# First pair of chunks by eight plain products, weights narrowed on VectorE alone, and the sums of squares queued behind the score products

## The chip, the cores and the metric

The kernel runs on one core of a Trainium2 chip. Its time is the device time of one execution in microseconds (us). The five engines work side by side, each through its own queue in order: TensorE (PE in the profile, with PEld for its weight loads), VectorE (DVE), ScalarE (ACT), GpSimd (POOL) and SyncE (SP), whose queue issues all the transfers here. A matrix product goes to a PSUM bank, and DVE or ACT take it from there.

## The reference

Four batches of a channel attention feed one Gelu layer pair. `q`, `k`, `v` have the shape (4, 6080, 256); everything is fp32, and the weights arrive as fp64.

```python
qn = q / (np.linalg.norm(q, axis=1, keepdims=True) + 1e-06)
kn = k / (np.linalg.norm(k, axis=1, keepdims=True) + 1e-06)
s = kn.transpose(0, 2, 1) @ qn / tau          # 256 x 256 per batch
a = softmax(s)                                # rows, with 1e-09 in the denominator
x = (v @ a).reshape(24320, 256)
h = x @ w_in                                  # 256 -> 2048
g = 0.5 * h * (1.0 + erf(h / sqrt(2)))
return g @ w_out                              # 2048 -> 256
```

The kernel multiplies `a` into `w_in` first (W = a @ w_in, 256 x 2048 per batch), so each batch is two large products around a Gelu, h = v @ W and out = g @ w_out.

## The kernel before

**Precision.** A product of two fp32 matrices is made of fp32r matmuls on a high and a low part of each operand: high by high, high by low and low by high, three matmuls for one product (`product`, L443, and L518 to L520). A split is a cast on ACT (`hi`) and a subtraction on DVE (`lo`). The products of the first batch's scores are plain fp32 (L147).

**The score stage (batch 0).** `qk_first(js)` runs for 24 steps `js`. A step takes a 512 KB block `raw` of `k` and `q` rows and adds four products to the two score blocks `s` in PSUM. For the first 16 steps (`NSQ`) `squares` squares the block on ACT and adds it on DVE to `acc`; the norms' remaining rows come from `norm_part`, which loads a piece `kq` of 1024 columns and sums its squares on ACT (L212). At step 18 (`NSQ + 2`) `sum_up` (L175) sums `acc` over the partitions by eight one-column products with a vector of ones, into `nps`. Blocks for 13 steps are loaded ahead; in the same queue of SP stand the `kq` pieces, the first `v` block, and the fp64 weight blocks ("units").

**The softmax** is a generator of stages; between them `qk_fill` gives PE the first four steps of the next batch's scores (16 products, L164). Stage one copies the scores from PSUM and adds the sums of squares, the next makes the reciprocal norms, then come the scaling with a product `rq` (L322), the exponential (L333), and transposes into `eh` and `el`.

**Weights.** `narrow(hi, lo, raw, eng)` makes an fp32r pair from one fp64 unit of 128 x 512 without fp64 arithmetic: clamp (L237), square on ACT (L239), shift and merge of the bits (L242, L244), a mask (L246), the exponent (L249), the tail (L251 on DVE, or L254 on ACT and L255 on POOL), a cast on ACT (L256), and two last steps on POOL (L257, L258). There are 16 units, eight of `w_in` (four groups of two) and eight of `w_out`; `NARROWS` says behind which score steps the first five are narrowed, and `paces` how many follow behind each unit of the first pair of chunks. Every third of these has its tail made on DVE (`VEC`). `keep` writes the pairs to DRAM for later chunks. Working tiles are `nt` at first, and `kqc` (two buffers) later.

`w_group(b, g)` multiplies `eh`, `el` with `win` for a quarter of the 2048 features (12 matmuls, L369 to L371), scales it out of PSUM into four blocks A11, A12, A21, A22 and forms the four sums S1 to S4. Seven of the eight, without A21, are split into `whs`, `wls`.

**Chunks.** The rows of a batch go in six pairs of chunks, each chunk up to 512 rows. `v_sums` forms T1 to T4 from the four blocks B of the pair's `v`, `v_split` splits the seven operands in `ORDER`. In `first_products` eight units `u` of 256 features each make the four blocks of h for two chunks by seven products instead of eight, a Strassen scheme in Winograd's form: three intermediate results are copied from PSUM by ACT (`p1`, `p5`, `u2`, L468) and added by DVE to later ones (`h`, L473). `gelu` makes `gh` and `g` on ACT (L456, L457) and `gl` on DVE (L458). Behind each product stands one group of three matmuls of the second layer for the unit before (`second_products`, L518 to L520).

**What sets the order.** The tile framework places each instruction in its engine's queue by program order and by its own estimate of readiness; single-buffered tiles and PSUM banks (four each for `ph` and `po`) add waits. `behind(name)` queues instructions behind a marked one, and `high_priority` puts the softmax and the first weight group forward. Transfers keep their order on SP, so a transfer that waits for a buffer holds those behind it.

Of the kernel before, what the change touches and what calls it, by code (L numbers as in the profile page):

```python
# [47 lines left out]

VEC = 3

TOP_MAX = (2.0 - 2.0 ** -3 - 2.0 ** -23) * 2.0 ** 16
TOP_MIN = 1.125 * 2.0 ** -15

A11, A22, A12, S1, S2, S3, S4 = range(7)
B11, B21, B22, T1, T2, T3, T4 = range(7)


@with_exitstack
def channel_attention_gelu_ffn(ctx, tc, qk, kqt, vt, tau, w_in, w_out, out):
# [80 lines left out]
    def qk_first(js):  # L140
        if js == 0:
            state["s"] = [bank()[:, 0:C] for m in range(NCT)]
        s = state["s"]
        raw = raws.pop((0, js))
        for j in range(JS):
            for m in range(NCT):
                nc.tensor.matmul(s[m], raw[:, j, 0, m * P:(m + 1) * P], raw[:, j, 1],  # L147
                                 start=(js == 0 and j == 0), stop=(js * JS + j == NJ - 1), skip_group_check=True)
# [74 lines left out]

    def narrow(hi, lo, raw, eng):

# [23 lines left out]
        nc.vector.tensor_scalar(out=body, in0=w.bitcast(U32), scalar1=0xFF800000, scalar2=None, op0=ALU.bitwise_and)  # L249
        if eng is nc.vector:  # L250
            eng.scalar_tensor_tensor(out=tail, in0=low, scalar=2.0 ** -52, in1=body.bitcast(F32), op0=ALU.mult,  # L251
                                     op1=ALU.mult)
        else:
            nc.scalar.activation(out=tail, in_=low, func=AF.Copy, scale=2.0 ** -52)  # L254
            eng.tensor_tensor(out=tail, in0=tail, in1=body.bitcast(F32), op=ALU.mult)  # L255
        nc.scalar.copy(out=hi, in_=w)  # L256
        nc.gpsimd.tensor_tensor(out=w, in0=w, in1=f32(hi), op=ALU.subtract)  # L257
        nc.gpsimd.tensor_tensor(out=lo, in0=w, in1=tail, op=ALU.add)  # L258

# [25 lines left out]
    def softmax(first, pool, name):  # L285
# [13 lines left out]
        nsum = state.pop("nsum")  # L299
        if first:  # L300
            nc.vector.reduce_sum(out=z, in_=nsum[:, :, NSQ // NSJ:NSC], axis=AX.X)
            nc.vector.tensor_tensor(out=x, in0=state.pop("nps")[:, 0:2 * NCT], in1=z, op=ALU.add)
        else:
            nc.vector.reduce_sum(out=x, in_=nsum[:, :, 0:NSC], axis=AX.X)
# [46 lines left out]


    def w_split(g, i, src):
        nc.scalar.copy(out=whs[g][:, i], in_=src)
        nc.vector.tensor_tensor(out=wls[g][:, i], in0=src, in1=f32(whs[g][:, i]), op=ALU.subtract)  # L355

    def w_group(b, g):
# [7 lines left out]
        for m in range(NCT):  # L365
            cs = slice(m * P, (m + 1) * P)
            pwt = bank()
            for d in range(NCT):
                nc.tensor.matmul(pwt, eh[:, d, cs], win[:, 0, d], start=(d == 0), stop=False)  # L369
                nc.tensor.matmul(pwt, eh[:, d, cs], win[:, 1, d], start=False, stop=False)  # L370
                nc.tensor.matmul(pwt, el[:, d, cs], win[:, 0, d], start=False, stop=(d == NCT - 1))  # L371
            nc.scalar.activation(out=tmp[:, 2 * m:2 * m + 2], in_=pwt.rearrange("p (q r c) -> p r q c", q=2, r=2),
                                 func=AF.Copy, scale=state["rden"][:, m:m + 1])
            if first and m == 0:
                w_split(g, A11, a11)
        tt = nc.vector.tensor_tensor
        if first:

            tt(out=s1, in0=a21, in1=a22, op=ALU.add)
            w_split(g, S1, s1)  # L380
            tt(out=s2, in0=s1, in1=a11, op=ALU.subtract)
            w_split(g, S2, s2)
            w_split(g, A12, a12)
            tt(out=s3, in0=a11, in1=a21, op=ALU.subtract)
            w_split(g, S3, s3)
            tt(out=s4, in0=a12, in1=s2, op=ALU.subtract)
            w_split(g, S4, s4)
            w_split(g, A22, a22)
# [38 lines left out]
    def v_split(b, p, i):  # L427
        n = PAIRS[p][1]
        x = v_blocks(b, p)
        src = {B11: x[0, 0], B21: x[1, 0], B22: x[1, 1]}.get(i)  # L430
        if src is None:
# [11 lines left out]
    def product(b, p, u, a, v, ps, start, stop):  # L443
        n = PAIRS[p][1]
        g, q = divmod(u, 2)
        hi, lo = vops[b, p, v]
        wh, wl = whs[g][:, a, q], wls[g][:, a, q]
        nc.tensor.matmul(ps[:, :n], wh, hi[:, :n], start=start, stop=False, skip_group_check=True)  # L448
# [3 lines left out]
    def gelu(src, n):  # L452
# [5 lines left out]
        nc.vector.tensor_tensor(out=gl[:, :n], in0=g[:, :n], in1=f32(gh[:, :n]), op=ALU.subtract)  # L458
        return gh, gl

    def first_products(b, p, u):
# [90 lines left out]

    def narrow_unit(eng):
        kind, g, d, raw = loaded.popleft()
        if kind == "in":
            if d == 0:
                new_win(0, g)
            win = wins[0, g]
            narrow(win[:, 0, d], win[:, 1, d], raw, eng)
            if d == NCT - 1:  # L560
                keep(keep_in[g], win)
        else:
            new_wo((0, 0, g))
            wo = wos[0, 0, g]
            narrow(wo[:, 0].rearrange("p f c -> p (f c)"), wo[:, 1].rearrange("p f c -> p (f c)"), raw, eng)
            keep(keep_out[g], wo)
# [5 lines left out]

    paces = (2, 1, 2, 2, 1, 1, 1)
    loaded = deque()
# [13 lines left out]
    for js in range(NQS):  # L588
# [7 lines left out]
        if js in NARROWS:  # L596
            narrow_unit(nc.gpsimd)
# [31 lines left out]
    load_unit()  # L629
    narrow_unit(nc.gpsimd)  # L630
    load_unit()
# [55 lines left out]
    for b, p, u in steps:  # L687
        pair = (b, p + 1) if p + 1 < NP else (b + 1, 0)
        for i, _ in enumerate(first_products(b, p, u)):
            next(second, None)  # L690
            if u == NU - 1 and pair[0] < B:
                v_split(*pair, ORDER[i][1])
# [4 lines left out]
        if (b, p) == (0, 0):  # L697
            for _ in range(paces[u] if u < len(paces) else 0):
                narrow_unit(nc.vector if len(units) % VEC == 0 else nc.gpsimd)
                if units:  # L700
# [33 lines left out]
```

## Time and profile before

| | |
|---|---|
| median of three runs | 2243.2 us (2242.62 to 2248.22) |
| the profiled execution | 2243.63 us, span 2241.8 us |
| granted TensorE clock, mean | 0.992 |
| busy: PE, DVE, ACT, POOL | 2190.7, 1410.7, 1451.9, 77.1 us |
| moved by transfers | 269.63 MB, mean 120 GB/s |

The span runs from the first instruction to the last; the rest of the execution's time lies around it. A busy PE need not be at its best rate: its records overlap, and at a lower granted clock they take longer. Where rows are shown, a timeline's columns are start, duration, engine, line, operation, tiles and shapes, with a count and, in brackets, the idle time before and what ended it; a group's are busy time and mean duration in nanoseconds, and then the idle time before. An x with a number is a count of instructions. An fp32 matmul leaves two records.

### The profile page before, as it was taken

The page shows a single profiled execution, that of the slowest core. Times are in us where ns is not written, and L with a number is a line of the kernel's source. Part 1 is how long each engine was busy: PE and PEld are TensorE (multiplying, and loading weights), DVE is VectorE, ACT ScalarE, POOL GpSimd, SP SyncE. Part 2 cuts the span into 40 slices and gives each one's busy share as a digit, 9 for nine tenths or more (in the row PEclk, how much of TensorE's full clock was granted, in tenths as well). Part 3 has the DMA queues.
Part 4 walks back from the last instruction along what each step waited for, and adds up shares of the span by engine and source line. Part 5 has one row for each costly group of instructions (what it writes and reads, how often), then busy time and mean ns, then how long its engine had stood idle before and what let it go on. Part 6 is the DMA issues. An engine that isn't in the chain of part 4 may idle for free.

```text
span 2241.8 us, 26294 instructions
## 1 busy us (share of the span) xinstructions
PE 2190.7 (98%) x9640; PEld 1795.2 (80%) x9640; DVE 1410.7 (63%) x2161; ACT 1451.9 (65%) x2637; POOL 77.1 (3%) x52
## 2 busy tenths in 40 slices
PE   7889999999999999999999999999999999999999
PEld 5667777888888888888888888888888888888888
DVE  6698466675666766756567666576566655555454
ACT  6467887565985656656666556566576666666665
POOL 3351000000000000000000000000000000000000
PEclk9899999999999999999999999999999999999999
DMA  9446766331573323323224232232122221221221
GB/s 349 176 149 217 229 231 211 109 116 62 187 237 111 123 85 104 122 82 105 76 94 138 87 123 103 85 121 81 62 86 84 90 88 48 94 85 51 90 68 53
DMA packets 77634, 269.63 MB, mean 120 GB/s; under 512 B 7744, under 2 KB 9792, under 8 KB 75456
## 3 DMA queue, kind: packets, MB, share of 16 engines
q1 hardware_dynamic: 77504, 267.94, 35.2%
q8 instruction: 76, 1.25, 0.2%
q14 instruction: 54, 0.44, 0.1%
HBM read 234.62 MB, written 33.29 MB: 120 GB/s over the span
## 4 chain that ended last, share of the span: by engine, by line
PE 80%; ACT 6%; DMA 4%; DVE 4%; issue 1%; POOL 0%; ACTq 0%; DVEq 0%; POOLq 0%
PE po L520 14%; PE po L518 13%; PE po L519 13%; PE ph L450 12%; PE ph L449 12%; PE ph L448 12%; DMA kqc<-kqt 4%; PE ph L194 2%; ACT kqc L212 2%; ACT gh L456 1%; ACT g L457 1%; PE ph L196 1%; DVE gl L458 1%; DVE h L473 1%; PE ph L370 0%
## 5 line engine op out<-in xcount | busy, mean ns | idle before, releaser
L458 DVE TENSOR_TENSOR gl<-g,gh 128x512 fp32r<-128x512 f32 (+1 forms) x768 | 529.0, 691 | 155.8 <-ACT g L457 152.9
L520 PE MATMUL po<-gh,wo 128*128 128x512 f32 (+1 forms) x1536 | 605.7, 394 | 0.0
L519 PE MATMUL po<-gl,wo 128*128 128x512 f32 (+1 forms) x1536 | 597.2, 389 | 3.3 <-DVE gl L458 3.3
L518 PE MATMUL po<-gh,wo 128*128 128x512 f32 (+1 forms) x1536 | 598.3, 390 | 0.0
L473 DVE TENSOR_TENSOR h<-ph,p 128x512 f32<-128x512 f32 (+1 forms) x384 | 262.5, 684 | 529.3 <-PE ph L450 415.4
L456 ACT ACTIVATE gh<-h 128x512 fp32r<-128x512 f32 (+1 forms) x576 | 360.7, 626 | 298.6 <-DVE h L473 295.8
L448 PE MATMUL ph<-vh,wh 128*128 128x512 f32 (+1 forms) x1344 | 528.3, 393 | 21.2 <-DVE h L473 8.9
L450 PE MATMUL ph<-vh,wl 128*128 128x512 f32 (+1 forms) x1344 | 527.3, 393 | 1.8 <-DVE wl L355 1.0
L449 PE MATMUL ph<-vl,wh 128*128 128x512 f32 (+1 forms) x1344 | 526.4, 392 | 0.0
L468 ACT COPY p<-ph 128x512 f32<-128x512 f32 (+1 forms) x384 | 222.4, 583 | 250.7 <-PE ph L450 250.4
L457 ACT ACTIVATE g<-h 128x512 f32<-128x512 f32 (+1 forms) x576 | 352.5, 612 | 0.0
L519 PEld LDWEIGHTS po<-gl,wo 128*128 128x128 f32 x1536 | 288.9, 188 | 69.6 <-DVE gl L458 5.6
L520 PEld LDWEIGHTS po<-gh,wo 128*128 128x128 f32 x1536 | 289.0, 188 | 61.4
L518 PEld LDWEIGHTS po<-gh,wo 128*128 128x128 f32 x1536 | 288.5, 188 | 61.8 <-ACT gh L456 0.6
L448 PEld LDWEIGHTS ph<-vh,wh 128*128 128x128 f32 x1344 | 253.5, 189 | 85.4 <-DVE h L473 13.3
L449 PEld LDWEIGHTS ph<-vl,wh 128*128 128x128 f32 x1344 | 253.8, 189 | 56.0
L450 PEld LDWEIGHTS ph<-vh,wl 128*128 128x128 f32 x1344 | 253.4, 189 | 54.4 <-DVE wl L355 1.4
L468 ACT COPY u<-ph 128x512 f32<-128x512 f32 (+1 forms) x192 | 111.6, 581 | 116.5 <-PE ph L450 116.5
L473 DVE TENSOR_TENSOR h<-ph,u 128x512 f32<-128x512 f32 (+1 forms) x192 | 131.1, 683 | 3.4
L457 ACT ACTIVATE g<-ph 128x512 f32<-128x512 f32 (+1 forms) x192 | 111.8, 582 | 0.0
L456 ACT ACTIVATE gh<-ph 128x512 fp32r<-128x512 f32 (+1 forms) x192 | 110.2, 574 | 0.0
L194 PE MATMUL ph<-hl 128*128 128x512 f32 x272 | 96.0, 392 | 0.0
(135 smaller groups left out, 1399.4 us busy)
## 6 DMA issues: line engine op xcount, KB each, us to landing
wo<-keep_out SPq DMA_DIRECT2D x184, 512.0 KB, 3.3
raw<-qk SPq DMA_DIRECT2D x95, 512.0 KB, 4.4
kqc<-kqt SPq DMA_DIRECT2D x72, 512.0 KB, 4.5
v_raw<-vt SPq DMA_DIRECT2D x20, 1024.0 KB, 5.0
out<-osb SPq DMA_DIRECT2D x40, 512.0 KB, 3.2
win<-keep_in SPq DMA_DIRECT2D x12, 1024.0 KB, 5.0
kq<-kqt SPq DMA_DIRECT2D x8, 512.0 KB, 7.6
raw<-w_out SPq DMA_DIRECT2D x8, 512.0 KB, 4.1
```

The costliest lines, as they stand in the source:

```text
L194: nc.tensor.matmul(s, hl[:, 0, j, 0, cs], hl[:, :, j, 1], start=(i == 0), stop=False, skip_group_check=True)
L448: nc.tensor.matmul(ps[:, :n], wh, hi[:, :n], start=start, stop=False, skip_group_check=True)
L449: nc.tensor.matmul(ps[:, :n], wh, lo[:, :n], start=False, stop=False, skip_group_check=True)
L450: nc.tensor.matmul(ps[:, :n], wl, hi[:, :n], start=False, stop=stop, skip_group_check=True)
L456: nc.scalar.activation(out=gh[:, :n], in_=src, func=AF.Gelu)
L457: nc.scalar.activation(out=g[:, :n], in_=src, func=AF.Gelu)
L458: nc.vector.tensor_tensor(out=gl[:, :n], in0=g[:, :n], in1=f32(gh[:, :n]), op=ALU.subtract)
L468: nc.scalar.copy(out=t[:, :n], in_=ps[:, :n])
L473: nc.vector.tensor_tensor(out=h[:, :n], in0=ps[:, :n], in1=t[:, :n], op=ALU.add)
L518: nc.tensor.matmul(o, wo[:, 0, i, cs], gh[:, :n], start=first, stop=False)
L519: nc.tensor.matmul(o, wo[:, 0, i, cs], gl[:, :n], start=False, stop=False)
L520: nc.tensor.matmul(o, wo[:, 1, i, cs], gh[:, :n], start=False, stop=last)
```

## The change

Three parts.

1. `sum_up` leaves step 18 of the scores. It is issued in the softmax's first stage, behind the mark `scores` that the last score product leaves.
2. `narrow` makes every tail on DVE (L251's form) and takes its two last steps from POOL to DVE. `paces` and the operands of `narrow_unit` follow.
3. The first pair of chunks of the first batch takes `plain_products`: eight products from A11, A12, A21, A22 and B11, B12, B21, B22, two to a block, with neither copies nor sums. So `v_sums` and three of the seven `v_split` fall away for this pair; `w_split` also makes A21 for the first batch's groups, in the tiles of T2 and T3 of the chunks (`w_slot`); and the first group's S sums are formed and split behind its four plain blocks. The later pairs are as before.

```diff
+A21, B12 = -1, T1
+PLAIN = (((1, 0), ((A11, B11), (A12, B21))), ((0, 0), ((A21, B11), (A22, B21))),
+         ((1, 1), ((A11, B12), (A12, B22))), ((0, 1), ((A21, B12), (A22, B22))))
...
-                nc.tensor.matmul(s[m], raw[:, j, 0, m * P:(m + 1) * P], raw[:, j, 1], ...
+                marks["scores"] = nc.tensor.matmul(
...
-        if js == NSQ + 2:
-            nps, acc = ps_o.tile([P, NT], F32, name="po"), state.pop("acc")
-            for j in range(JS):
-                sum_up(nps, acc[:, j], j == 0, j == JS - 1)
-            state["nps"] = nps
...
-        if eng is nc.vector:
-            eng.scalar_tensor_tensor(out=tail, in0=low, scalar=2.0 ** -52, in1=body.bitcast(F32), op0=ALU.mult,
-                                     op1=ALU.mult)
-        else:
-            nc.scalar.activation(out=tail, in_=low, func=AF.Copy, scale=2.0 ** -52)
-            eng.tensor_tensor(out=tail, in0=tail, in1=body.bitcast(F32), op=ALU.mult)
+        nc.vector.scalar_tensor_tensor(out=tail, in0=low, scalar=2.0 ** -52, in1=body.bitcast(F32), op0=ALU.mult,
+                                       op1=ALU.mult)
         nc.scalar.copy(out=hi, in_=w)
-        nc.gpsimd.tensor_tensor(out=w, in0=w, in1=f32(hi), op=ALU.subtract)
-        nc.gpsimd.tensor_tensor(out=lo, in0=w, in1=tail, op=ALU.add)
+        nc.vector.tensor_tensor(out=w, in0=w, in1=f32(hi), op=ALU.subtract)
+        nc.vector.tensor_tensor(out=lo, in0=w, in1=tail, op=ALU.add)
...
         if first:
+            nps, acc = ps_o.tile([P, NT], F32, name="po"), state.pop("acc")
+            with behind("scores"):
+                for j in range(JS):
+                    sum_up(nps, acc[:, j], j == 0, j == JS - 1)
...
+    def w_slot(g, i):
+        if i != A21:
+            return whs[g][:, i], wls[g][:, i]
+        if g // 2 not in w21:
+            w21[g // 2] = [pv.tile([P, 2, 2, P], F32R, name=f"v{x}{T2 + g // 2}") for x in "hl"]
+        return [t[:, g % 2] for t in w21[g // 2]]
...
-            if first and m == 0:
-                w_split(g, A11, a11)
+            if first:
+                for i in ((A11, A21), (A12, A22))[m]:
+                    w_split(g, i, {A11: a11, A12: a12, A21: a21, A22: a22}[i])
         tt = nc.vector.tensor_tensor
-        if first:
...
-            return
+        if b == 0 and not first:
+            w_split(g, A21, a21)
...
         for to, of in ((slice(0, 3), slice(1, 4)), (slice(3, 7), slice(4, 8))):
+            if first and to.start == 0:
+                continue
...
+    def plain_products(b, p, u):
+        n = PAIRS[p][1]
+        out = state["blocks"] = {}
+        for at, terms in PLAIN:
+            ps = bank()
+            for i, (a, v) in enumerate(terms):
+                product(b, p, u, a, v, ps, i == 0, i == 1)
+                if i == 1:
+                    out[at] = gelu(ps[:, :n], n)
+                if len(out) < 4:
+                    yield
...
-    paces = (2, 1, 2, 2, 1, 1, 1)
+    paces = (1, 2, 1, 2, 2, 1, 1)
...
-        if js in (10, 11):
-            v_sums(0, 0, js - 10)
-        if 12 <= js < 19:
-            v_split(0, 0, ORDER[js - 12][1])
+        if 12 <= js < 16:
+            v_split(0, 0, (B11, B21, B12, B22)[js - 12])
...
-        for i, _ in enumerate(first_products(b, p, u)):
+        products = plain_products if (b, p) == (0, 0) else first_products
+        for i, _ in enumerate(products(b, p, u)):
             next(second, None)
-            if u == NU - 1 and pair[0] < B:
+            if u == NU - 1 and pair[0] < B and i < 6:
                 v_split(*pair, ORDER[i][1])
```

More of the change, by code (lines that the diff above doesn't have):

```diff
@@ L146, in qk_first @@
             for m in range(NCT):
-                nc.tensor.matmul(s[m], raw[:, j, 0, m * P:(m + 1) * P], raw[:, j, 1],
-                                 start=(js == 0 and j == 0), stop=(js * JS + j == NJ - 1), skip_group_check=True)
+                marks["scores"] = nc.tensor.matmul(
+                    s[m], raw[:, j, 0, m * P:(m + 1) * P], raw[:, j, 1],
+                    start=(js == 0 and j == 0), stop=(js * JS + j == NJ - 1), skip_group_check=True)
         if js < NSQ:
             squares(js, raw)
-        if js == NSQ + 2:
-            nps, acc = ps_o.tile([P, NT], F32, name="po"), state.pop("acc")
-            for j in range(JS):
-                sum_up(nps, acc[:, j], j == 0, j == JS - 1)
-            state["nps"] = nps
     def qk_fill():
@@ L222, in load_w, with narrow @@
         return raw
-    def narrow(hi, lo, raw, eng):
+    def narrow(hi, lo, raw):
         n = raw.shape[1]
@@ L350, in softmax @@
         state["e"], state["rden"] = (eh, el), rden
+    w21 = {}
+    def w_slot(g, i):
[4 more added lines that the diff above has]
+        return [t[:, g % 2] for t in w21[g // 2]]
     def w_split(g, i, src):
-        nc.scalar.copy(out=whs[g][:, i], in_=src)
-        nc.vector.tensor_tensor(out=wls[g][:, i], in0=src, in1=f32(whs[g][:, i]), op=ALU.subtract)
+        hi, lo = w_slot(g, i)
+        nc.scalar.copy(out=hi, in_=src)
+        nc.vector.tensor_tensor(out=lo, in0=src, in1=f32(hi), op=ALU.subtract)
     def w_group(b, g):
@@ L430, in v_split @@
         src = {B11: x[0, 0], B21: x[1, 0], B22: x[1, 1]}.get(i)
+        if (b, p, i) == (0, 0, B12):
+            src = x[0, 1]
         if src is None:
@@ L558, in narrow_unit @@
             win = wins[0, g]
-            narrow(win[:, 0, d], win[:, 1, d], raw, eng)
+            narrow(win[:, 0, d], win[:, 1, d], raw)
             if d == NCT - 1:
```

25 lines of the change are left out of this document (7 added, 18 removed).

## The prediction

> **What bounds the kernel now.** I read the page's busy shares and slices first, then the stretches (busy time by window) of the first 203 us, then the timeline of each engine there, and last the groups by shape, to price single operations.
>
> ```profile
> span 2241.8 us, 26294 instructions
> ...
> PE 2190.7 (98%) x9640; PEld 1795.2 (80%) x9640; DVE 1410.7 (63%) x2161; ACT 1451.9 (65%) x2637; POOL 77.1 (3%) x52
> ...
> POOL 3351000000000000000000000000000000000000
> PEclk9899999999999999999999999999999999999999
> ```
>
> TensorE (PE) is busy for all but 51.1 us of the span, so only its idle time and its slow records can be won; every added matmul costs its full price. GpSimd (POOL) works in the first four slices alone, and the clock's one dip (8) lies among them. The next answer counts PE, PEld, DVE, ACT and POOL busy time, then the granted clock and the DMA share.
>
> ```profile
> 40.00:42.00 2.00, 1.78 (x9) 1.22 (x7) 2.00 (x3) 1.62 (x3) 0.00 (x0) 1.00 0.64 207
> 42.00:46.00 4.00, 0.00 (x0) 0.00 (x0) 3.34 (x6) 3.05 (x5) 2.27 (x2) 1.00 0.96 368
> 46.00:50.00 4.00, 0.00 (x0) 0.00 (x0) 3.79 (x3) 4.00 (x8) 3.92 (x2) 0.58 0.53 155
> 50.00:60.00 10.00, 8.68 (x29) 7.64 (x30) 2.91 (x10) 4.11 (x9) 0.08 (x1) 0.50 1.02 390
> ...
> 77.50:203.00 125.50, 101.77 (x390) 76.31 (x390) 113.96 (x167) 82.75 (x151) 58.15 (x35) 0.92 0.40 139
> 203.00:403.00 200.00, 195.00 (x853) 155.84 (x852) 125.25 (x192) 164.15 (x311) 0.00 (x0) 1.00 0.69 228
> ```
>
> There are two places. Stage A, to 77.5 us, is the score product and softmax: PE stands still from 41.8 us and then runs at half clock (0.50). Stage B, 77.5 to 203 us, is the first pair of chunks with the narrowing of the weights. In the stretch after it 853 matmuls take 195.00 us, 0.2286 each; at that price stage B's 390 need 89.2 of its 125.5 us. The other 36.3 are 23.7 idle (125.5 - 101.77) and 12.6 of slow clock. VectorE (DVE) is the full engine: 113.96 us of 125.5, 91%.
>
> **Stage A, the sums of squares.**
>
> ```profile
> 29.03 12.75 PE L147 MATMUL ph<-raw 128*128 128x256 f32 x56 [0.56 <-DMA raw<-qk]
> 51.32 3.54 PE L175 MATMUL po<-ones,acc 128*128 128x1 f32 x16 [9.54 <-DVE acc L137]
> ...
> 54.72 15.06 PE L147 MATMUL ph<-raw 128*128 128x256 f32 x56
> 69.62 3.19 PE L164 MATMUL po<-raw 128*128 128x256 f32 x14
> ...
> 77.50 0.50 PE L369 MATMUL ph<-win,eh 128*128 128x512 f32 x1
> ...
> SPq L211 <- ACT kq L212: 13.4, 4, 5.1
> ...
> 49.53 2.68 SPq L121 DMA_DIRECT2D raw<-qk  x5
> ...
> raw<-qk SPq DMA_DIRECT2D x9, 512.0 KB, 7.5
> ```
>
> In PE's queue `sum_up` (L175) stands in the middle of the scores and waits 9.54 us for DVE's last `acc`; the 56 score records behind it, seven steps of eight, run partly cold and end at 54.72 + 15.06 = 69.8. Behind the last score product the wait is gone. Late next is either PE or the data. PE: 41.8 + 12.75 (the earlier 56 records at full clock) = 54.5. Data: step 23 is the first of the five loads issued at 49.53 (the other four are the next batch's); plus 7.5 to landing and 1.8 for its eight records is 58.9. The loads themselves were held: SP waited 13.4 us for `kq` buffers that ACT frees, and ACT trailed DVE. Before 52 us the change takes four `v_sums` and three splits off DVE and adds nine narrowing operations of 0.6 us (5.4), while POOL's overlap, priced below, goes. So I take the middle, 56.7, a gain of 13.1 (10.9 to 15.3).
>
> What comes back: `sum_up`'s 16 records now lie between the last score and the fill. They cost 3.5 at half clock; I take 1.8 (half, on a warm array), bounds 1.7 and 3.5. The chain behind it (DVE 56.51 to 58.5 below, with ACT's square root in it) has the seven fill matmuls, 14 records and 3.19 us, over it; if they were gone it would cost about 2.1. From the fill on, everything to 77.5 is the same sequence. Stage A gains **11.3 us** (7.4 to 13.6).
>
> ```profile
> 56.51 0.16 DVE L302 TENSOR_TENSOR small<-po,small 128x4 f32<-128x4 f32 x1
> ...
> 58.31 0.22 DVE L319 TENSOR_SCALAR small<-small,rtau 128x2 f32<-128x2 f32 x1
> ```
>
> **Stage B, narrowing without GpSimd.** In groups by shape (busy, mean ns) of 77 to 203 us, and the last row of 204 to 400 us, where POOL is idle:
>
> ```profile
> L458 DVE TENSOR_TENSOR gl<-g,gh 128x512 fp32r<-128x512 f32 x31 | 27.5, 893 | 1.7 <-ACT g L457 1.5
> L473 DVE TENSOR_TENSOR h<-ph,p 128x512 f32<-128x512 f32 x16 | 10.7, 680 | 1.3 <-PE ph L450 1.3
> L244 DVE SCALAR_TENSOR_TENSOR raw<-raw,kqc 128x512 uint32<-128x512 uint32 x11 | 10.2, 928 | 0.0
> L242 DVE TENSOR_SCALAR kqc<-raw 128x512 uint32<-128x512 uint32 x11 | 8.0, 737 | 7.6 <-POOL wo L258 3.8 <-POOL win L258 3.7
> ...
> L237 DVE TENSOR_SCALAR raw<-raw 128x512 f32<-128x512 f32 x11 | 7.8, 714 | 0.0
> L473 DVE TENSOR_TENSOR h<-ph,u 128x512 f32<-128x512 f32 x8 | 5.4, 678 | 0.0
> ...
> L423 DVE TENSOR_TENSOR vs<-v_raw,vs 128x512 f32<-128x512 f32 x1 | 1.8, 1815 | 0.0
> ...
> L237 DVE TENSOR_SCALAR raw_w<-raw_w 128x512 f32<-128x512 f32 x1 | 0.4, 425 | 0.0
> ...
> L458 DVE TENSOR_TENSOR gl<-g,gh 128x512 fp32r<-128x512 f32 x67 | 46.2, 689 | 26.8 <-ACT g L457 26.1 <-PE ph L450 0.3
> ```
>
> Beside POOL `gl` takes 893 ns instead of 689, L244 928 instead of about 690, L242 and L237 737 and 714 instead of 425, one `vs` sum 1815. `h`, whose one input lies in PSUM, is not stretched. These rows alone give 31 x 0.204 + 11 x (0.238 + 0.312 + 0.289) + 1.1 = 16.6 us; the smaller groups should carry some more (an estimate: half as much at most), so I take 21 (16.6 to 25) of DVE time that goes with POOL's 58.15.
>
> What it costs: POOL's 35 operations in this stretch become 35 DVE operations, since nine more tails are made by L251 and 26 are the two last steps. Neighbouring DVE records start 0.60 apart (next fence): 35 x 0.60 = 21.0 us. The two nearly cancel on DVE. What does not cancel is latency, as here:
>
> ```profile
> 118.85 0.68 DVE L473 TENSOR_TENSOR h<-ph,p 128x512 f32<-128x512 f32 x1
> 119.45 0.68 DVE L473 TENSOR_TENSOR h<-ph,u 128x512 f32<-128x512 f32 x1
> ...
> 132.62 5.46 POOL L255 TENSOR_TENSOR kqc<-kqc,raw 128x512 f32<-128x512 f32 x1 [5.90 <-ACT wo L256]
> ...
> 140.75 1.51 DVE L242 TENSOR_SCALAR kqc<-raw 128x512 uint32<-128x512 uint32 x1 [3.83 <-POOL wo L258]
> ...
> 143.58 0.68 DVE L473 TENSOR_TENSOR h<-ph,p 128x512 f32<-128x512 f32 x1
> ...
> 147.92 0.79 PE L448 MATMUL ph<-vh,wh 128*128 128x512 f32 x1 [6.29 <-DVE h L473]
> 148.51 0.63 PE L449 MATMUL ph<-vl,wh 128*128 128x512 f32 x1
> ...
> 93.18 0.80 PE L370 MATMUL ph<-win,eh 128*128 128x512 f32 x1 [3.25 <-POOL win L258]
> ```
>
> POOL's three steps hold a scratch buffer; DVE's L242 waits for it, `h` is queued behind L242, and PE waits 6.29 us for `h` and then runs slow (0.63 a record). At 93.18 it waits 3.25 us for POOL itself. After the change the last writer is DVE, two 0.60 us steps behind the cast.
>
> SP and POOL's queue: `keep` and the loads behind it on SP wait for DVE instead of POOL, hence earlier; POOL's queue keeps its memsets only.
>
> **Stage B, plain products.** PE: eight units, one product of three matmuls more each: 24 x 0.2286 = +5.5 us, wholly on the path. DVE: 24 `h` sums go (the 16 and 8 above): 24 x 0.60 = -14.4; the `A21` splits of groups 1 to 3 and the first group's later S splits add about 1.2. ACT loses the copies `p`, `u` and nine narrowing copies; at 82.75 of 125.5 us that is no term. With four plain blocks a Gelu follows its second product directly instead of the chain copy, add, Gelu.
>
> The first group: before, products waited for A11, S1, S2 one behind another; now the four blocks need only their own split, and the S splits come later under pair 0.
>
> At the seam to the second chunk pair: `A21` lies in the T2 and T3 tiles and B12 in T1's, all single buffers. T1 and T3 of the next pair can be written only behind unit 7's seventh product. T1 is needed five groups of three matmuls later (15 x 0.2286 = 3.4 us), and copy and subtract need about 1.2. Covered, it costs nothing, without the cover up to 3.4; I take 0.7, near the covered end because 3.4 is well over 1.2.
>
> Sums: PE floor 89.2 + 5.5 = 94.7. DVE floor 113.96 - 21 - 14.4 + 21.0 + 1.2 = 100.8. DVE stays the nearer one, and as units differ in load neither floor is reached. Before, DVE was idle for 9% of the stage; with the same share 100.8 / 0.91 = 110.8, but waits on POOL (L242's 7.6 us) were most of that share, so I take half: 100.8 / 0.955 = 105.5. **Gain 20.0 us.** Ends: 96.8 if the stretch was 25 and DVE never waits (gain 28.7); and PE floor plus the old losses less the two waits above, 9.5, and the slow records behind them, about 4: 94.7 + 36.3 - 13.5 = 117.5 (gain 8.0).
>
> ```profile
> 84.68 0.79 PE L448 MATMUL ph<-vh,wh 128*128 128x512 f32 x1 [1.34 <-ACT wh L354]
> 85.27 0.63 PE L449 MATMUL ph<-vl,wh 128*128 128x512 f32 x1
> ```
>
> On the slow records: they come not only behind the 3.25 and 6.29 us waits but already here, behind a wait of 1.34 us in a stretch of several. So short waits of the first unit can still cost clock after the change, and I leave such records in the upper end. The Trainium skill ("TensorE: Matmul & The Clock Gate", What's actually happening) says that the array falls to half clock after an idle window of about 3.4 us; no single wait here is that long, so the trace differs from it. By that rule waits below 3.4 us would add no slow records, and the seven of this place (about 0.2 us each) would come off the upper end, 1.4 us.
>
> **Sum.** 2243.6 (the profiled execution: 2241.8 span and 1.8 around it; 0.4 above the runs' median) - 11.3 - 20.0 + 0.7 (seam) = 2213. After 203 us PE is busy 195 of 200 us and nothing is timed by a clock, so the gain is passed on to the end. Adding ends with ends, the range is 2243.6 - 42.3 = 2201 to 2243.6 - 15.4 = 2228.
>
> **Rivals.** (1) DVE is the bound of stage B and the work moved onto it eats the relief: narrowing comes in bursts (two units are 8 us), `gl` waits behind them and PE behind `gl`. For it: 91% DVE. Against it: 14.4 us of `h` go. It gives the worse end of B, perhaps less: 2243.6 - 11.3 - 6 = 2226. A sentence of the Trainium skill ("Perfetto Trace Analysis", Optimizing Scalar/DVE Operations) points here: with a saturated DVE some work may be better on Scalar or GpSimd, though the page adds that sharing a read port it may not help. (2) The stretch is not POOL's doing and stays: B's DVE floor is 121.8, over 0.955 127.5, 2 us more than before; with A 2234. Against it: `gl` is 689 where POOL is idle, and `h` is 680 throughout. (3) Slower: on DVE each narrowing, now 4.0 us (five 0.60 and three of about 0.34), stands whole in front of the `gl` that PE needs next. PE then waits 13 x 4.0 = 52 us; all old waits (36.3) and A's 11.3 are spent when the waits pass 42.1 us (47.6 - 5.5), 3.2 us per narrowing. At the full price it is 2253. Against it: units take PE 11 us and PE has two groups' work in hand. (4) Stage A's gain doesn't arrive, since the loads stay late and the third weight block's data then sets unit 0: A gives 3, 2220.
>
> **How the numbers follow.** The forecast 0.66 (its own range 2203 to 2224), rival 1 0.17, rival 4 0.07, rival 2 0.04, rival 3 0.06. About 0.3%, 6.7 us, is what a measurement here can tell from no change. All but rival 3 end more than that below 2243, but near rival 2 some mass lies within it: faster 0.92, same 0.03, slower 0.05. Low 2203 and high 2229 leave out rivals 2 and 3 and the far ends.
>
> **What would show it.** No PE wait for `acc`, scores ending near 57 and the first L369 near 66; POOL idle after the first microseconds; `gl` at 0.69 and L242 at 0.42 throughout; stage B about 105 us from its first L369 to the corresponding point, with 24 more matmuls. Wrong: PE waits on `gl` or on the split of `wl` beyond 12 us in stage B, a score end beyond 59, or a PE wait at the seam.

## The result and the profile after

The changed kernel takes 2208.24 us (median of four runs, 2206.87 to 2209.85) where the kernel before, on the same chip, takes 2243.57. The ratio is 0.9839, with an interval of 0.9822 to 0.9856. A second series on another chip gave 0.9842 (0.9816 to 0.9869). The forecast was 2213. One execution of a kernel further down (narrowing alone) took 4403.84 us, twice as long as its three others, and is left out of its figures.

The page of the changed kernel, its head, busy shares and the clock by slices:

```profile
span 2206.5 us, 26233 instructions
...
PE 2182.0 (99%) x9664; PEld 1792.7 (81%) x9664; DVE 1387.1 (63%) x2175; ACT 1432.3 (65%) x2599; POOL 1.3 (0%) x8
...
PEclk9999999999999999999999999999999999999999
```

The dip in the clock is gone, and so is GpSimd's work but for eight short operations, 1.3 us together. For stage A and stage B I use the same two marks in every kernel from here on: S is the start of the first product of the first weight group, T the start of the 168th product record of the second layer (the end of the group behind unit 6). Stage B is S to T. The stretches of the kernel before, by these marks (start and end, length, then busy time and count of PE, PEld, DVE, ACT, POOL, the granted clock, the DMA share and GB/s):

```profile
0.00:77.50 77.50, 60.86 (x247) 50.37 (x247) 44.12 (x62) 39.66 (x62) 18.92 (x17) 0.91 0.90 346
77.50:201.79 124.29, 100.56 (x384) 75.32 (x384) 112.78 (x165) 81.54 (x148) 58.15 (x35) 0.92 0.41 139
```

And of the kernel after:

```profile
0.00:64.73 64.73, 56.46 (x247) 44.88 (x247) 38.25 (x65) 36.67 (x56) 1.31 (x8) 1.00 0.99 386
64.73:166.12 101.39, 96.03 (x409) 77.55 (x408) 94.88 (x176) 65.80 (x119) 0.00 (x0) 0.98 0.57 190
```

Stage A is 12.8 us shorter (77.50 to 64.73), stage B 22.9 (124.29 to 101.39), and 0.4 comes back later: 35.3 in all, the difference of the two profiled executions (2243.63 and 2208.33). In stage B PE's idle time falls from 23.7 us (124.29 - 100.56) to 5.4 (101.39 - 96.03), a gain of 18.4; PE's busy time falls by another 4.5 although it makes 24 matmuls more (5.5 us), so some 10 us of slow records went too.

PE's timeline of the kernel after:

```profile
28.47 26.99 PE L149 MATMUL ph<-raw 128*128 128x256 f32 x112 [0.57 <-DMA raw<-qk]
55.30 1.84 PE L172 MATMUL po<-ones,acc 128*128 128x1 f32 x16
57.00 3.27 PE L161 MATMUL po<-raw 128*128 128x256 f32 x14
...
64.73 0.58 PE L377 MATMUL ph<-win,eh 128*128 128x512 f32 x1
...
68.93 0.50 PE L450 MATMUL ph<-vh,wh 128*128 128x512 f32 x1 [1.07 <-ACT wh L362]
69.27 0.40 PE L451 MATMUL ph<-vl,wh 128*128 128x512 f32 x1
...
79.04 0.80 PE L533 MATMUL po<-gh,wo 128*128 128x512 f32 x1 [4.30 <-ACT gh L458]
...
80.12 0.63 PE L378 MATMUL ph<-win,eh 128*128 128x512 f32 x1
...
180.28 0.50 PE L450 MATMUL ph<-vh,wh 128*128 128x512 f32 x1 [0.64 <-ACT p L483]
```

The last 112 score records run as one block and end at 55.46 (28.47 + 26.99), with a granted clock of 1.00 throughout, and `sum_up` (L172) follows without a wait. In stage B two waits are left of all those of before: 1.07 us for the first split of the weight group, that of A11, and 4.30 us for the first Gelu.

VectorE's groups by shape in stage B after, and from its timeline of stage A the row of the last `acc`:

```profile
L460 DVE TENSOR_TENSOR gl<-g,gh 128x512 fp32r<-128x512 f32 x30 | 20.5, 685 | 3.2 <-ACT g L459 3.1
L241 DVE SCALAR_TENSOR_TENSOR raw<-raw,kqc 128x512 uint32<-128x512 uint32 x11 | 7.5, 685 | 0.0
...
L239 DVE TENSOR_SCALAR kqc<-raw 128x512 uint32<-128x512 uint32 x11 | 4.5, 418 | 0.0
```

```profile
42.55 1.23 DVE L139 TENSOR_TENSOR acc<-acc,sq 128x1024 f32<-128x1024 f32 x1 [0.45 <-ACT sq L138]
```

`gl` is back at 685 ns (893 before), the merge (L241) at 685 (928), the shift (L239) at 418 (737). The last `acc` is ready at 43.8, before at 51.2.

### The profile page after: what moved, and what is told of

The parts are those of the page before. It is cut to its first block, busy times and chain, and to the rows that moved or that the text cites. A ratio compares the mean times of both kernels' runs of the same rounds, so it can differ in the third digit from the quotient of the medians.

```text
span 2206.5 us, 26233 instructions
## 1 busy us (share of the span) xinstructions
PE 2182.0 (99%) x9664; PEld 1792.7 (81%) x9664; DVE 1387.1 (63%) x2175; ACT 1432.3 (65%) x2599; POOL 1.3 (0%) x8
## 4 chain that ended last, share of the span: by engine, by line
PE 87%; ACT 6%; DMA 5%; DVE 2%; issue 0%; SPq 0%; ACTq 0%; DVEq 0%
PE po L535 15%; PE po L533 14%; PE po L534 14%; PE ph L452 13%; PE ph L451 13%; PE ph L450 12%; DMA kqc<-kqt 4%; PE ph L191 2%; ACT kqc L209 2%; ACT gh L458 1%; ACT g L459 1%; PE ph L193 1%; DMA raw<-qk 1%; DVE acc L139 1%; PE ph L377 1%; PE ph L379 1%
## 5 line engine op out<-in xcount | busy, mean ns | idle before, releaser
L460 DVE TENSOR_TENSOR gl<-g,gh 128x512 fp32r<-128x512 f32 (+1 forms) x768 | 522.8, 682 | 157.7 <-ACT g L459 155.5
L488 DVE TENSOR_TENSOR h<-ph,p 128x512 f32<-128x512 f32 (+1 forms) x368 | 251.6, 684 | 526.0 <-PE ph L452 415.2
L458 ACT ACTIVATE gh<-h 128x512 fp32r<-128x512 f32 (+1 forms) x552 | 345.7, 626 | 285.0 <-DVE h L488 281.8
L450 PE MATMUL ph<-vh,wh 128*128 128x512 f32 (+1 forms) x1336 | 522.1, 391 | 7.6 <-ACT p L483 3.2
L483 ACT COPY p<-ph 128x512 f32<-128x512 f32 (+1 forms) x368 | 213.2, 583 | 247.7 <-PE ph L452 247.5
L459 ACT ACTIVATE g<-h 128x512 f32<-128x512 f32 (+1 forms) x552 | 337.6, 612 | 0.0
L458 ACT ACTIVATE gh<-ph 128x512 fp32r<-128x512 f32 (+1 forms) x216 | 124.9, 578 | 22.9 <-PE ph L452 22.7
L488 DVE TENSOR_TENSOR h<-ph,u 128x512 f32<-128x512 f32 (+1 forms) x184 | 125.6, 683 | 3.4
L459 ACT ACTIVATE g<-ph 128x512 f32<-128x512 f32 (+1 forms) x216 | 126.3, 585 | 0.0
```

The lines of the kernel that those rows point to most:

```text
L458: nc.scalar.activation(out=gh[:, :n], in_=src, func=AF.Gelu)
L459: nc.scalar.activation(out=g[:, :n], in_=src, func=AF.Gelu)
L483: nc.scalar.copy(out=t[:, :n], in_=ps[:, :n])
L488: nc.vector.tensor_tensor(out=h[:, :n], in0=ps[:, :n], in1=t[:, :n], op=ALU.add)
```

## The experiments

The theory after the result: GpSimd's work cost stage B about 20 us, through waits and stretched records in the chains that feed PE, and the sums of squares cost stage A about 10. The main rival was the prediction's own ledger: VectorE's total load sets stage B, so the plain products, which take 24 sums off it, carry the gain. The first three kernels do one part alone, the next three leave one part out.

**One part alone: the sums of squares.** Against the kernel before:

```diff
-        if js == NSQ + 2:
-            nps, acc = ps_o.tile([P, NT], F32, name="po"), state.pop("acc")
-            for j in range(JS):
-                sum_up(nps, acc[:, j], j == 0, j == JS - 1)
...
+            nps, acc = ps_o.tile([P, NT], F32, name="po"), state.pop("acc")
+            with behind("scores"):
+                for j in range(JS):
+                    sum_up(nps, acc[:, j], j == 0, j == JS - 1)
```

> Part 1 alone: the sums of squares behind the last score product, all else as before. Theory (the three parts share the gain): the 9.54 us wait and the cold clock go, but VectorE is still stretched by GpSimd before 52 us, so the loads stay late and the scores end near 58.9 instead of 69.8; with 1.8 for the sums the first weight group starts near 68.5, 9 us earlier, and stage B is unchanged: 2234.5. Rival (stage A's wait is hidden by what follows, the narrowing of the second weight group): the start moves but the gain is lost in the first unit, 2241 to 2243.

Measured 2232.44 us, ratio 0.9961 (0.9946 to 0.9976). Its stretches:

```profile
0.00:68.11 68.11, 57.23 (x246) 46.12 (x247) 44.21 (x63) 39.81 (x62) 18.94 (x17) 0.97 0.95 361
68.11:192.01 123.90, 102.38 (x385) 77.54 (x384) 111.43 (x165) 81.19 (x148) 59.37 (x35) 0.90 0.44 157
```

All of it is stage A, 9.4 us; stage B keeps its 124. The scores end at 58.85, as expected, with a wait of 2.79 us for data in front of the last 24 records.

**One part alone: narrowing without GpSimd.** Against the kernel before:

```diff
-        nc.gpsimd.tensor_tensor(out=w, in0=w, in1=f32(hi), op=ALU.subtract)
-        nc.gpsimd.tensor_tensor(out=lo, in0=w, in1=tail, op=ALU.add)
+        nc.vector.tensor_tensor(out=w, in0=w, in1=f32(hi), op=ALU.subtract)
+        nc.vector.tensor_tensor(out=lo, in0=w, in1=tail, op=ALU.add)
...
-    paces = (2, 1, 2, 2, 1, 1, 1)
+    paces = (1, 2, 1, 2, 2, 1, 1)
```

> Part 2 alone: narrowing without GpSimd, seven products, sums of squares still at step 18. Theory: acc is ready near 44 us instead of 51, so PE waits about 2 us at step 18 and stays warm: stage A gains about 11 without part 1. In stage B VectorE's floor stays 114 (minus 21 of stretch, plus 21 of moved work) and only the waits on GpSimd go, a gain of about 5: 2227 in all. Rival (what matters in stage B is the plain products, and narrowing on a VectorE that is already 91% busy gives nothing back): stage B gets slower by up to 6 and the total is 2238 or more.

Measured 2218.08 us (the middle of three), ratio 0.9893 (0.9876 to 0.9909), two thirds of the whole gain. Its stage B:

```profile
72.44:177.22 104.78, 95.36 (x382) 72.52 (x381) 100.84 (x190) 73.59 (x136) 0.00 (x0) 0.95 0.39 136
```

Stage B is 19.5 us shorter. VectorE has 25 records more there (190 for 165) and is yet busy 11.9 us less. Counted by shape, 33 of the 35 moved operations lie in the stage, and eight other records, among them four splits of the next batch's blocks, have left it. At the mean durations that the same shapes have in this kernel, the 165 records of the kernel before would last about 25 us less in sum (an estimate from the groups by shape of both): that stretch went with GpSimd. The prediction's ledger gives this kernel 114 us of VectorE work in stage B (113.96 - 21 + 21.0) and hence a gain of about 5 there; the measured gain is four times that. Stage A gains 5.1 us (72.44), less than half of what was expected: the wait for `acc` shrinks to 4.69 us, not to 2, and the records behind it are still slow.

**One part alone: plain products.** Against the kernel before (with `w_slot`, the four plain splits and the later S splits):

```diff
-        for i, _ in enumerate(first_products(b, p, u)):
+        products = plain_products if (b, p) == (0, 0) else first_products
+        for i, _ in enumerate(products(b, p, u)):
```

> Part 3 alone: plain products in the first pair of chunks, GpSimd still narrows, sums of squares at step 18. Theory: stage A gains about 5, since four sums and three splits leave VectorE before 52 us; stage B gains about 10, since 13 us of VectorE work go but its stretch of about 20 and the waits on GpSimd stay, and PE has 5.5 us more: 2228. Rival (the plain products alone make stage B's gain): stage B takes about 102 us and the total is 2215 or less.

Measured 2239.77 us, ratio 0.9994 (0.9984 to 1.0003): no change that can be told. The gain of about 10 us expected in stage B is not there:

```profile
74.27:201.67 127.40, 106.38 (x409) 82.42 (x408) 93.67 (x141) 69.03 (x126) 66.57 (x35) 0.91 0.39 136
```

This is the row that decides against the ledger. VectorE is busy 93.67 us in stage B, as after the whole change (94.88), PE has the same matmuls, and yet the stage takes 127.40 us instead of 101.39. VectorE's load cannot be what differs; GpSimd's 66.57 us is. (The profiled execution is the slowest of ten, 5.7 us above their median. Even if all of that lies in stage B, some 20 us remain.)

**Left out: the sums of squares.** The kernel after with `sum_up` back at step 18:

```diff
+        if js == NSQ + 2:
+            nps, acc = ps_o.tile([P, NT], F32, name="po"), state.pop("acc")
+            for j in range(JS):
+                sum_up(nps, acc[:, j], j == 0, j == JS - 1)
...
-            with behind("scores"):
-                for j in range(JS):
-                    sum_up(nps, acc[:, j], j == 0, j == JS - 1)
```

> Parts 2 and 3 without part 1. Theory: once VectorE is not stretched, acc is ready when PE reaches step 18, give or take 2 us, and moving the sums is worth next to nothing: 2209 to 2211. Rival (moving the sums is what gains stage A): the wait stays and with it most of stage A's 12.8 us, 2217 to 2221.

Measured 2210.69 us, ratio 0.9863 (0.9848 to 0.9878). Its stretches, and from PE's timeline the first record of `sum_up`:

```profile
0.00:67.45 67.45, 59.00 (x246) 48.17 (x246) 38.12 (x64) 36.47 (x56) 1.31 (x8) 0.97 0.98 387
67.45:170.15 102.70, 97.25 (x409) 78.23 (x408) 95.03 (x177) 65.88 (x118) 0.00 (x0) 0.97 0.51 176
```

```profile
43.99 1.92 PE L176 MATMUL po<-ones,acc 128*128 128x1 f32 x16 [1.94 <-DVE acc L139]
```

With VectorE relieved by the other two parts, the wait for `acc` is 1.94 us, not 9.54. So the part that alone is worth 9.4 us in stage A adds 2.7 there on top of the others (67.45 against 64.73), and the intervals of the times overlap with those of the whole change.

**Left out: narrowing without GpSimd.** The kernel after with `narrow` as before (the two `nc.gpsimd` lines, the copy of the tail on ACT, `paces`):

```diff
-        nc.vector.tensor_tensor(out=w, in0=w, in1=f32(hi), op=ALU.subtract)
-        nc.vector.tensor_tensor(out=lo, in0=w, in1=tail, op=ALU.add)
+        nc.gpsimd.tensor_tensor(out=w, in0=w, in1=f32(hi), op=ALU.subtract)
+        nc.gpsimd.tensor_tensor(out=lo, in0=w, in1=tail, op=ALU.add)
```

> Parts 1 and 3 without part 2: GpSimd narrows again. Theory: stage A gains 9 to 11, stage B about 10 of its 22.9, since stretch and waits on GpSimd stay: 2223 to 2225. gl in stage B takes about 0.85 us a record. Rival (stage B's gain is the plain products' alone): 2209 to 2212.

Measured 2233.79 us, ratio 0.9958 (0.9943 to 0.9973): some 27 us of the gain go with this one part. None of stage B's gain is left, where 10 us were expected. Stage B by window, and rows of the waits in it (engine and line, what it waited for, us in total, times, longest):

```profile
67.77:192.83 125.06, 106.06 (x410) 82.71 (x409) 100.42 (x141) 68.97 (x125) 64.15 (x35) 0.90 0.43 152
```

```profile
ACT kqc L238 <- POOL win L257: 9.7, 2, 5.4
...
ACT kqc L238 <- POOL wo L257: 8.0, 3, 3.0
...
PE ph L456 <- ACT g L465: 8.4, 2, 4.4
...
SPq L220 <- POOL kqc L254: 29.2, 5, 11.6
```

VectorE is idle for 24.6 us of the stage (125.06 - 100.42). PE's two waits for a Gelu (L465) have different causes. The first, 4.41 us at 142.60, goes back to a GpSimd operation that was held up:

```profile
126.01 9.33 POOL L254 TENSOR_TENSOR kqc<-kqc,raw 128x512 f32<-128x512 f32 x1 [3.16 <-ACT kqc L253]
135.31 1.29 POOL L256 TENSOR_TENSOR kqc<-kqc,win 128x512 f32<-128x512 f32 x1
...
139.30 1.51 DVE L236 TENSOR_SCALAR raw<-raw 128x512 f32<-128x512 f32 x1 [5.12 <-DMA raw<-w_out]
```

The tail's product (L254) took 9.33 us where GpSimd's next operation took 1.29. It reads the `raw` block, so SP's next load of a weight block waited 11.6 us for it, and VectorE then 5.12 us for that load. ACT's squares of the next units (L238) waited for GpSimd's last write (5.4 us) and for VectorE, the Gelus stood behind them in ACT's queue, and PE waited for the Gelus. The second wait, 4.00 us at 158.21, has the same queue in it, but ACT's square there starts right behind VectorE's clamp of that unit (L236), which VectorE reached late: six of its records, from 145.09 on, took 1.50 to 1.79 us each.

**Left out: plain products.** The kernel after with seven products for the first pair, so parts 1 and 2:

```diff
-        products = plain_products if (b, p) == (0, 0) else first_products
-        for i, _ in enumerate(products(b, p, u)):
+        for i, _ in enumerate(first_products(b, p, u)):
```

> Parts 1 and 2 without part 3: seven products, VectorE narrows. Theory: stage A gains its 12.8; stage B has VectorE at about 114 us of clean work and takes about 119, a gain of 5: 2226. Rival (PE is the bound, and the eighth product costs its 5.5 us): stage B takes about 96 and the total is 2203.

Measured 2212.85 us, ratio 0.9868 (0.9853 to 0.9883); stage B:

```profile
64.47:169.49 105.02, 94.95 (x382) 72.71 (x381) 100.70 (x190) 73.46 (x136) 0.00 (x0) 0.95 0.45 157
```

That lies between the two expectations. On top of the other two the plain products take 3.6 us off stage B (105.02 to 101.39), and the intervals of the two kernels' ratios just touch. VectorE is busy for 96% of the stage here (100.70 of 105.02), so without GpSimd it may well be near the bound, which no run tests. The eighth product costs its 5.5 us of PE, but PE's idle time falls from 10.1 to 5.4 us and the clock rises from 0.95 to 0.98.

**GpSimd's work added back, with a result that nobody reads.** The kernel after with three additions on GpSimd for each narrowed unit, into a spare tile that nothing else reads (the tile of T4, which the first pair doesn't need):

```diff
+        spare = f32(state["spare"])
+        for _ in range(3):
+            nc.gpsimd.tensor_tensor(out=spare, in0=f32(hi), in1=spare, op=ALU.add)
```

> The changed kernel with GpSimd work that nobody needs: behind each cast three additions of 128x512 fp32 into a spare tile, 48 in all, as many as the narrowing gave to GpSimd at most; no engine waits for them. Theory (the stretch is GpSimd's): gl in stage B goes from 0.68 to 0.8 us or more, VectorE's 95 us in a stage of 101 grow by about 20, and PE waits for it: 2217 to 2225. Rival (the stretch had another cause, such as the seven products' pattern): gl stays 0.68 and the time 2208.

Measured 2256.72 us, ratio 1.0064 (1.0049 to 1.0079): slower than the kernel before, and far more than expected. Stage B by window; three of VectorE's groups; the waits:

```profile
72.44:205.59 133.15, 103.38 (x410) 81.19 (x408) 122.12 (x171) 59.66 (x108) 95.00 (x38) 0.87 0.39 135
```

```profile
L466 DVE TENSOR_TENSOR gl<-g,gh 128x512 fp32r<-128x512 f32 x28 | 23.2, 833 | 0.0
L247 DVE SCALAR_TENSOR_TENSOR kqc<-raw 128x512 f32<-128x512 uint32 x11 | 10.7, 975 | 0.0
...
L239 DVE TENSOR_SCALAR kqc<-raw 128x512 uint32<-128x512 uint32 x11 | 5.6, 512 | 0.0
```

```profile
ACT wo L249 <- POOL vh L255: 12.0, 1, 12.0
DVE raw L234 <- DMA raw<-w_out: 10.7, 1, 10.7
...
PE ph L456 <- ACT g L465: 9.5, 1, 9.5
...
PE po L541 <- DVE wo L257: 8.7, 1, 8.7
```

The same VectorE records stretch (685 to 833, 683 to 975, 418 to 512), 122.12 us of them for 94.88. That the stretch is GpSimd's doing is shown. Its price is not: the spare additions read `hi`, so they also hold a weight tile and what is to be written or loaded there (ACT waits 12.0 us for one of them, and VectorE 10.7 us for a load that stands on SP behind another, which waits 17.4 us for GpSimd). PE's wait of 9.5 us, at 159.40, comes from that load. Its wait of 8.7 us, at 170.57, ends with the last of nine stretched VectorE records in a row, 1.49 to 1.76 us each from 155.91 on.

**A third scratch buffer with GpSimd.** If the price is the loop through two scratch buffers, a third should free it. The kernel without part 2, with every third unit in the spare tiles:

```diff
+            state["nth"] = state.get("nth", -1) + 1
+            if state["nth"] % 3 == 2:
+                w, tail = (f32(pv.tile([P, NT], F32R, name=f"v{c}{T4}")) for c in "hl")
```

> Parts 1 and 3 with GpSimd narrowing, as without part 2, but every third unit behind the fill has a scratch buffer of its own (in T4's idle tiles), so three instead of two units can be under way. Theory (with GpSimd the narrowing chain sets stage B by its latency: a unit holds its scratch buffer for 14.6 us from its shift to its last write, two buffers give one unit in 7.3 us): stage B falls from 125 us to 110 to 115, 2220 to 2224. Rival (it is the stretched VectorE records and their order, not the buffers): stage B stays at 122 to 126, 2230 to 2235.

Measured 2233.34 us, ratio 0.9955 (0.994 to 0.997), as without it. Stage B by window; one of the waits; part of VectorE's timeline:

```profile
67.56:190.68 123.12, 102.97 (x410) 79.36 (x408) 104.46 (x141) 69.12 (x125) 61.21 (x35) 0.94 0.44 157
```

```profile
PE ph L465 <- DVE wl L409: 5.0, 1, 5.0
```

```profile
98.69 1.50 DVE L402 TENSOR_TENSOR hl<-hl 128x256 f32<-128x256 f32 x1
100.11 1.48 DVE L403 TENSOR_TENSOR hl<-hl 128x256 f32<-128x256 f32 x1
101.51 2.01 DVE L409 TENSOR_TENSOR wl<-hl,wh 128x768 fp32r<-128x768 f32 x1
103.44 1.50 DVE L404 TENSOR_TENSOR hl<-hl 128x256 f32<-128x256 f32 x1
```

The buffer theory fell. What remains is visible here at one place: GpSimd works from 95.05 to 104.66 us almost without a pause, three sums of a weight group take 1.48 to 1.50 us (0.42 after the change) and the split between them 2.01 (0.95), and PE waits 5.00 us for that split, `wl`. The excess of L402, L403 and L409 alone is 3.2 us (1.50 + 1.48 + 2.01 - 0.42 - 0.42 - 0.95). So what a stretched record costs here lies not in VectorE's total but in its place in a chain that PE waits for.

**One scratch buffer without GpSimd.** The kernel after with all of stage B's units in one pair of tiles instead of two buffers:

```diff
-            tmp = pg.tile([P, 2, n], F32, name="kqc", bufs=2)
+            w, tail = (f32(pv.tile([P, NT], F32R, name=f"v{c}{T4}")) for c in "hl")
```

> The changed kernel with one scratch buffer instead of two for the narrowing behind the fill. Theory (the buffer loop sets the pace when it is slow enough): a unit holds its buffer 9.0 us, eleven units in a row take 99 us, and stage B grows by 8 to 15 us, 2216 to 2223. Rival (the narrowing has slack on VectorE alone): within 2 us of 2208.

Measured 2210.31 us, ratio 0.9853 (0.9827 to 0.9879); stage B takes 102.23 us, 0.8 more than with two:

```profile
64.61:166.84 102.23, 97.01 (x409) 78.11 (x408) 95.71 (x177) 65.84 (x118) 0.00 (x0) 0.97 0.54 189
```

With the narrowing on VectorE, scratch space doesn't limit it.

**The last long wait.** PE's 4.30 us at 79.04 ends the chain narrowing, ACT, Gelu. ACT's timeline of the kernel after:

```profile
77.83 0.67 ACT L236 ACTIVATE kqc<-raw 128x512 f32<-128x512 f32 x1 [2.58 <-DVE win L251]
78.40 0.59 ACT L458 ACTIVATE gh<-ph 128x512 fp32r<-128x512 f32 x1
```

The first Gelu stands behind a narrowing's square that waits for VectorE. Loading two weight blocks earlier moves it:

```diff
+        if js == 13:
+            load_unit()
+            load_unit()
```

> The changed kernel with the two weight blocks of the second group loaded ahead of the last two blocks of the next batch's scores instead of behind them, so that they land 2.5 us earlier. Theory (the one long PE wait left, 4.30 us at 79 us, is for the narrowing of that group, behind which the first Gelu's buffers come free): the wait shrinks by about 2.5 us and some slow records go with it, 2204 to 2206. Rival (VectorE's sum of work up to the first Gelu sets it, not the landing): no change, 2208.

Measured 2206.3 us, ratio 0.984 (0.9823 to 0.9856), while the change itself has 0.9839. It was run again beside the change itself, on one chip:

> The changed kernel once more, on the chip of the next one, for a direct comparison: 2208 in all theories, 0.984 of before.

> The kernel with the two weight blocks of the second group loaded ahead, on the same chip as the changed kernel. Theory (its profile's stage B of 96.2 us instead of 101.4 is passed on to the end): 3.5 to 5 us less than the changed kernel. Rival (the gain of the profile is given back later, the medians being 2206.3 and 2208.2 on two chips): less than 2 us.

The changed kernel has 2207.91 us there, this one 2207.72, ratio 0.9838 (0.9813 to 0.9862). Stage B of the latter, and the stretch behind it; then the same stretch of the changed kernel:

```profile
64.33:160.53 96.20, 95.99 (x413) 77.44 (x414) 93.95 (x174) 64.67 (x115) 0.00 (x0) 1.00 0.56 198
...
166.03:1000.00 833.97, 826.15 (x3669) 675.89 (x3668) 535.79 (x817) 568.49 (x1047) 0.00 (x0) 1.00 0.44 145
```

```profile
166.03:1000.00 833.97, 829.30 (x3691) 678.73 (x3690) 538.68 (x823) 573.37 (x1055) 0.00 (x0) 1.00 0.44 146
```

In stage B it does what it should: 96.20 us with PE busy for 95.99, T 5.5 us earlier (160.53 against 166.03). But it is given back: to 1000 us PE is idle for 7.8 us instead of 4.7, mostly waits for ACT's copies, and from T on the profiled executions take 2043.3 against 2036.9 us. That rest also differs by 3.5 us between two executions of the changed kernel itself (2206.5 - 166.12 = 2040.4 and 2202.9 - 166.03 = 2036.9), so half of what is given back may be scatter. No kernel here clearly beats the changed one.

## Why the prediction was right, and where its working was not

The time was 4.8 us under the forecast, within its own range, and both stages came as forecast in sign and nearly in size. Step by step:

- **Stage A, 11.3 forecast, 12.8 measured.** The scores end at 55.46, not 56.7 (14.3 for the term of 13.1); `sum_up` puts back 1.7 us (55.30 to 57.00) for the term of 1.8; the first weight product starts at 64.73, not near 66. What the forecast didn't see is that the parts overlap: part 1 alone gives 9.4, parts 2 and 3 alone 5.1 and 3.2 (stage A of 72.44 and 74.27 us), together 12.8. The wait for `acc` goes when `sum_up` is moved, and it also shrinks when VectorE is relieved: from 9.54 to 4.69 us by part 2, to 6.43 by part 3, to 1.94 by both.
- **Stage B, 20.0 forecast, 22.9 measured; the size came near by a wrong step, so that part was luck.** The step that failed is "DVE stays the nearer one". VectorE's floor wasn't what held the stage before: with the same VectorE load it took 127.40 us beside GpSimd and 101.39 without. As a sum the floor wasn't far off (100.8 for the 94.88 us that VectorE is busy, with a stretch of about 25 for 21), but by it the plain products bring 13.2 us and the narrowing next to nothing. The runs show it the other way round: on top of the other parts, narrowing without GpSimd is worth 23.7 us of stage B (125.06 to 101.39) and the plain products 3.6. Of their 13.2 us only 5.8 show in VectorE's busy time (100.70 to 94.88), since records that lie behind T without them, among them four splits of the next batch's blocks, lie in front of it with them. After the change PE is the nearer floor: 96.03 us busy in 101.39, beside a PE floor forecast of 94.7. In the last experiment it is reached, 95.99 of 96.20.
- **"What does not cancel is latency"** was the right step, costed only as half of VectorE's idle share. Part 2 alone is worth 19.5 us of stage B, where the ledger would have given it about 5. The row that the prediction shows for it, GpSimd's 5.46 us at 132.62, is a held operation too: VectorE's records follow without a pause until 136.91, and it ends at 138.08.
- **The seam**, 0.7: PE waits 0.64 at 180.28, though for an ACT copy and not for T1's split.
- **Slow records.** After the change the clock drops behind the 4.30 us wait (0.63 a record at 80.12) and not behind the 1.07 us one (0.40 at 69.27). By the rule quoted from the Trainium skill ("TensorE: Matmul & The Clock Gate", What's actually happening) that is as it should be; the drop behind 1.34 us in the kernel before stays outside it.
- **Rivals.** (1) VectorE as the bound: PE never waits on `gl` in stage B after, and VectorE is idle for 6.5 us. The sentence that pointed there, of the Trainium skill ("Perfetto Trace Analysis", Optimizing Scalar/DVE Operations), holds here only by its proviso: taking work off GpSimd and onto a VectorE that was 91% busy gave 1.1%. (2) The stretch is GpSimd's: 685, 685 and 418 ns without it, 833 (`gl`) with spare work. (3) PE doesn't wait for a `gl` that stands behind a narrowing; its only long wait, 4.30, is for a Gelu behind one narrowing. (4) Stage A's gain arrived: the loads run at 0.99 of their engines, before at 0.90.

That part 2 is worth some 20 us of stage B is shown: with GpSimd narrowing the stage took 123.90 to 127.40 us in four kernels, without it 101.39 to 105.02 in the four that differ from these by part 2 alone. What stays open is how that price divides. Held GpSimd operations and stretched VectorE records are each shown behind single long waits of PE; no run takes one away and keeps the other, and each variant also shifts the static order of the queues. `paces` and the nine copies on ACT went with part 2 in every kernel, so their own share was not measured.

## What to carry to other kernels

An engine that is 91% busy isn't the bound until a kernel with less work on it is faster: here 19 us less of it moved nothing as long as GpSimd stayed in the narrowing. Look for an operation on a slow engine inside a chain that ends at the bottleneck, and price the whole chain at the longest time that this operation takes beside the others, not the engine's sum. Gains that remove the same wait don't add, and a few us won in one stage are won only if the rest of the program keeps its own time.

## What was not expected of the hardware

A mean duration hides two cases. The run with spare work shows both:

```profile
117.79 28.27 POOL L255 TENSOR_TENSOR vh<-win,vh 128x512 f32<-128x512 f32 x1 [9.85 <-ACT win L249]
...
143.03 0.68 DVE L466 TENSOR_TENSOR gl<-g,gh 128x512 fp32r<-128x512 f32 x1
...
157.59 1.75 DVE L466 TENSOR_TENSOR gl<-g,gh 128x512 fp32r<-128x512 f32 x1
```

In the first, VectorE is busy without a pause and its `gl` takes 0.68 us as in the kernel after, but one GpSimd addition lasts 28.27 us. It ends at 146.06, 1.15 us after VectorE's last record before a pause (144.91). The 9.33 us operation of the run without part 2 ends 1.16 us after such a point, and the 5.46 us one of the kernel before 1.17 us. With VectorE idle the next ones take 1.26 to 1.37 us. So in these three places GpSimd's operation was held as long as VectorE went on without a pause. In the second case GpSimd's operations follow each other, six in 9.43 us from 157.20 on, and VectorE's records grow instead, `gl` to 1.75 and, in the run with the third buffer, a sum of 128 x 256 more than threefold (0.42 to 1.50). What decides between the two cases is not shown here.

95 us of GpSimd work that feeds nothing, with the tiles that it holds, turned a gain of 1.6% into a loss of 0.6%.
